# Batch 0 of a spectral mixer: transform products of two output thirds set around the token products, mirrored relus put off

## The chip, the cores and the metric

The kernel runs on one core of one Trainium2 chip. The metric is the device time of one execution in microseconds. The profile's span is about 2 us shorter than that time (592.4 against 594.3 for the kernel before, in the profiled execution); times of day within an execution ("at 32.17") count from the start of the span.

## The reference

For each of 8 batches of 3008 tokens by 256 channels: the real part of a 2-D Fourier transform, then a token-mixing and a channel-mixing perceptron, each with a residual.

```python
def _attn_ref(x):
    X = np.fft.fft(x, axis=1)
    X = np.fft.fft(X, axis=2)
    return X.real.astype(np.float32)

def _moe_ref(x, w_tok1, w_tok2, w_ch1, w_ch2):
    xt = x.transpose(0, 2, 1)
    h = np.maximum(xt @ w_tok1, 0.0) @ w_tok2      # 3008 -> 256 -> 3008
    u = x + h.transpose(0, 2, 1)
    h2 = np.maximum(u @ w_ch1, 0.0) @ w_ch2        # 256 -> 1536 -> 256
    return (u + h2).astype(np.float32)
```

## The kernel before

The instruction order of every engine is the order of the program text. A batch's columns are worked in six chunks of 512 (`NCH`). Three "thirds" of the transform `yt`, each good for one chunk and, mirrored, for another, are made by eight 128-column products each: four into `pq`, four into `py`. ScalarE copies `pq` to `qs`, and VectorE makes the two halves of `yt` from `py` and `qs` (I call this the join).

The program uses eight buffers of PSUM, where TensorE's products land, shared out as three rings: `f` (3), `mm` (3) and `o2` (2). A ring's buffer can be written again only when its last reader is done.

```python
    def ps_mm(name, dt=FP32, n=512):
        return psum.tile([P, n], dt, tag="mm", name=name, bufs=3)
    def ps_out(name, dt=FP32, n=512):
        return psum.tile([P, n], dt, tag="o2", name=name, bufs=2)
    def ps_f(name, dt=FP32, n=512):
        return psum.tile([P, n], dt, tag="f", name=name, bufs=3)
    # ... cut ...
        def relu(th, uv, which=(0, 1, 2)):
            for i in which:          # 1 and 2 are the mirrored ones, wanted from chunk 3 on
                o, x = ((uu[:, th, 0, :, :], uv[:]),
                        (uu[:, th, 1, :, 1:P], uv[:, :, 1:P]),
                        (uu[:, th, 1, :, 0], uv[:, ::-1, 0]))[i]
                nc.scalar.activation(out=o, in_=x, func=AFT.Relu)

        def third(c, then=None):
            py, pq = ps_f("py"), ps_f("pq")
            for o, f, tab in ((pq, 131, tq), (py, 1, tp)):
                for k in range(4):
                    g = 4 * c + k
                    nc.tensor.matmul(o[:, P * k:P * k + P], lhsT=w[:, g, f:f + P],
                                     rhs=tab[:, g, :], start=True, stop=True)
            qs = perb.tile([P, CW], FP32, tag="qs", name="qs", bufs=2)
            nc.scalar.activation(out=qs[:], in_=pq[:], func=AFT.Copy)
            # ... cut ...
            for h, op in ((0, AT.subtract), (1, AT.add)):
                nc.vector.tensor_tensor(out=yt[:, h, CW * c:CW * c + CW], in0=py[:],
                                        in1=qs[:], op=op)
        # ... cut: batch 0 makes third 0, tok1 and the first relus ...
        for c in range(NCH):
            if c in (1, 2):
                third(c)
                yield
            # ... cut ...
            if (b, c) == (0, 0):
                pus = [ps_f("pu") for _ in range(2)]
                # ... cut: identity products put yt into pus (start=True, stop=False) ...
                for th in range(2):
                    for h in range(2):
                        nc.tensor.matmul(pus[h][:], lhsT=uu[:, th, 0, h, :],
                                         rhs=w2_cols(b, c)[:, th],
                                         start=False, stop=(th == 1))
                for h in range(2):
                    copy(1 - h, ut[:, h, :]..., pus[h][:]...)   # h=0 VectorE, h=1 ScalarE
                for th in range(2):
                    relu(th, uvs[th], (1, 2))
                yield
                continue
            for h in range(2):       # every other chunk
                pu = ps_f("pu")
                # ... cut: two products (the token products) ...
                nc.vector.tensor_tensor(out=ut[:, h, 0:n]..., in0=pu[:, 0:n]..., in1=y..., op=AT.add)
                yield

    def mm1(b, c, c1, cts):          # a group of three channel tiles
        for i in cts:
            pc = ps_mm("pc")
            for h in range(2):
                nc.tensor.matmul(pc[:, 0:n], lhsT=wc[:, h, ct * P:(ct + 1) * P],
                                 rhs=ut[:, h, 0:n], start=(h == 0), stop=(h == 1))
            if i not in (2, 8) or (b, c) != (0, 0):
                nc.scalar.activation(out=c1[:, ct, 0:n], in_=pc[:, 0:n], func=AFT.Relu)
            else:                    # tiles 2 and 8 of chunk 0: VectorE
                ts(c1[:, ct, 0:n], pc[:, 0:n], 0.0, AT.max)
```

The main loop puts out a group `mm1` of three channel tiles, then a step (up to a `yield`) of the generator above, and so on. A step is, for instance, a third, or one token product pair `pu`.

## Time and profile before

| | kernel before |
|---|---|
| time, median of 3 runs | 594.20 us (594.19 to 594.73) |
| TensorE busy | 98% |
| VectorE, ScalarE, GpSimd busy | 77%, 74%, 26% |
| TensorE idle listed in the whole span | 8.1 us in six waits, 5.9 of it at the very start |
| of that on lines that the change touches | 0.52 us at 31.65 |

The lines that carry this are in the prediction. One more stretch of TensorE's timeline matters later: the fourth group of channel tiles, chunk 2's token products and the first group of chunk 1.

```profile
37.99 1.46 PE L773 MATMUL pc<-ut,wc1p 128*128 128x512 f16 x6
39.29 0.59 PE L730 MATMUL pu<-w2p,uu 128*128 128x512 f16 x2
39.72 1.46 PE L773 MATMUL pc<-ut,wc1p 128*128 128x512 f16 x6
...
41.44 1.47 PE L888 MATMUL po<-wc,c 128*128 128x256 f16 x12
```

Read such rows by their starts. The length of a row includes the modelled end of its last matmul and overlaps the next row by some 0.16 us. Six products cost 39.29 - 37.99 = 1.30 us, two with `w2p` 0.43 us.

### The profile page before, as it was taken

The numbers are of one execution on the slowest core, as the hardware profiler recorded it, in microseconds if no ns is written. First come the engines' busy times: TensorE is split into PE (matmuls) and PEld (weight loads), VectorE is DVE, ScalarE is ACT, GpSimd is POOL, SyncE is SP. The second block draws the span as 40 slices with busy tenths as digits, with TensorE's granted clock in tenths as the row PEclk, the third lists the DMA queues.
The fourth block names the chain that finished last, engine by engine and source line by source line (L and its number), as shares of the span: only waits on it lengthen the run. The fifth ranks groups of instructions, "written<-read, shape, count | busy, mean of one in ns | idle before, by whom it ended". The sixth has DMA issues, their size and how long they took to land.

```text
span 592.4 us, 15959 instructions
## 1 busy us (share of the span) xinstructions
PE 580.4 (98%) x6397; PEld 419.8 (71%) x6397; DVE 458.7 (77%) x1075; ACT 437.7 (74%) x994; POOL 152.7 (26%) x251
## 2 busy tenths in 40 slices
PE   5999999999999999999999999999999999999997
PEld 4846777767776777676777667767777777866676
DVE  8868689878896887769797787868888677676573
ACT  7775887887778777777767776777777867766772
POOL 7530421412151211421134111421211121112131
PEclk9999999999999999999999999999999999999999
DMA  9996851863367242844329432492233335333424
GB/s 151 211 187 126 139 101 46 150 122 54 66 122 139 55 88 56 157 71 98 64 49 170 98 65 55 90 172 54 56 76 63 78 55 97 48 72 72 82 58 105
DMA packets 86683, 56.55 MB, mean 95 GB/s; under 512 B 54945, under 2 KB 83553, under 8 KB 85857
## 3 DMA queue, kind: packets, MB, share of 16 engines
q1 hardware_dynamic: 77984, 37.77, 33.6%
q0 software_dynamic: 8320, 17.49, 17.2%
q8 instruction: 50, 0.82, 0.6%
q10 hardware_dynamic: 304, 0.26, 0.2%
q14 instruction: 25, 0.20, 0.1%
HBM read 34.98 MB, written 24.64 MB: 101 GB/s over the span
## 4 chain that ended last, share of the span: by engine, by line
PE 96%; DVE 2%; ACT 1%; issue 0%; POOL 0%; DVEq 0%; POOLq 0%
PE pc L773 41%; PE px L817 25%; PE py L817 10%; PE pu L730 7%; PE pt L613 4%; PE po L888 2%; PE pz L518 2%; PE pq L645 1%; PE py L645 1%; PE py L836 1%; PE pw L596 1%; PE pw L597 1%; PE pw L560 0%; ACT z L307 0%; PE ph L430 0%; PE ph L432 0%
## 5 line engine op out<-in xcount | busy, mean ns | idle before, releaser
L776 ACT ACTIVATE c<-pc 128x512 f16<-128x512 f32 (+1 forms) x574 | 297.9, 595 | 31.3 <-PE pc L773 16.3
L799 POOL TENSOR_TENSOR osb<-osb,rt 128x256 f32<-128x256 f32 (+1 forms) x92 | 84.5, 919 | 373.3 <-DVE osb L799 366.1
L817 PEld LDWEIGHTS <-c 128*128 128x128 f16 x2112 | 128.1, 98 | 24.9
L773 PE MATMUL pc<-ut,wc1p 128*128 128x512 f16 x576 | 140.0, 379 | 0.5 <-DVE ut L305 0.5
L773 PE MATMUL pc<-ut,wc1m 128*128 128x512 f16 (+1 forms) x576 | 134.9, 370 | 0.0
L822 ACT ACTIVATE m<-px 128x256 f32<-128x256 f32 (+1 forms) x138 | 51.8, 375 | 75.4 <-PE px L817 46.0
L817 PEld LDWEIGHTS <-sb 128*128 128x128 f16 x1584 | 94.6, 98 | 10.4
L738 DVE TENSOR_TENSOR ut<-pu,yt 128x512 f16<-128x512 f32 (+1 forms) x94 | 63.3, 674 | 40.6 <-PE pu L730 40.3
L773 PEld LDWEIGHTS <-wc1p 128*128 128x128 f16 x576 | 52.0, 97 | 49.2 <-DMA wc1p<-in_moe_w_ch_dram,ixc 0.8
L773 PEld LDWEIGHTS <-wc1m 128*128 128x128 f16 x576 | 52.9, 98 | 45.0
L817 PE MATMUL px<-wst,c 128*128 128x128 f16 x1056 | 74.0, 219 | 0.0
L817 PE MATMUL px<-wc,c 128*128 128x128 f16 x1056 | 66.5, 219 | 0.0
L799 DVE TENSOR_TENSOR osb<-py,m 128x256 f32<-128x256 f32 (+1 forms) x92 | 37.5, 407 | 26.5 <-ACT m L822 26.2
L790 DVE TENSOR_TENSOR sb<-sb,c 128x768 f16<-128x768 f16 (+1 forms) x92 | 54.2, 589 | 3.2
L730 PE MATMUL pu<-w2p,uu 128*128 128x512 f16 (+1 forms) x184 | 54.7, 379 | 0.0
L790 DVE TENSOR_TENSOR sb<-c 128x768 f16<-128x768 f16 (+1 forms) x92 | 50.6, 550 | 0.0
L790 DVE TENSOR_TENSOR c<-c 128x768 f16<-128x768 f16 (+1 forms) x92 | 50.5, 548 | 0.0
L790 DVE TENSOR_TENSOR sb<-c,sb 128x768 f16<-128x768 f16 (+1 forms) x92 | 50.4, 548 | 0.0
L307 ACT ACTIVATE z<-pz 128x480 f16<-128x480 f32 (+1 forms) x60 | 39.0, 666 | 5.4 <-PE pz L527 3.0
L599 DVE SCALAR_TENSOR_TENSOR w<-alt,pw 128x131 f16<-128x131 f16 x84 | 29.2, 351 | 16.5 <-ACT w L307 16.0
L652 DVE TENSOR_TENSOR yt<-py,qs 128x512 f16<-128x512 f32 x48 | 30.9, 685 | 10.5 <-ACT qs L648 10.2
L817 PE MATMUL py<-wst,sb 128*128 128x128 f16 x528 | 37.1, 219 | 0.0
(201 smaller groups left out, 648.1 us busy)
## 6 DMA issues: line engine op xcount, KB each, us to landing
out_dram<-osb SPq DMA_DIRECT2D x83, 256.0 KB, 3.8
xp<-in_x_dram POOLq DMA_DIRECT2D x16, 272.0 KB, 5.3
out_dram<-osb SPq DMA_DIRECT2D x11, 192.0 KB, 3.1
xp<-in_x_dram POOLq DMA_DIRECT2D x16, 127.5 KB, 5.8
rt<-ut SPq DMA_TRANSPOSE x96, 3.8
w2s<-in_moe_w_tok_dram POOLq DMA_DIRECT2D x1, 1504.0 KB, 14.8
w1p<-in_moe_w_tok_dram POOLq DMA_DIRECT2D x4, 192.0 KB, 7.9
wc<-in_moe_w_ch_dram POOLq DMA_DIRECT2D x1, 768.0 KB, 15.2
```

What stands on the lines that cost most here:

```text
L307: nc.scalar.activation(out=out_, in_=in_, func=AFT.Copy)
L599: nc.vector.scalar_tensor_tensor(out=w[:, g, 0:131], in0=alt[:], scalar=pw[:, 131:132], in1=pw[:, 0:131], op0=AT.mult, op1=AT.add)
L613: nc.tensor.matmul(pt[:, o:o + n], lhsT=hw[:, g, th * P:th * P + P], rhs=w[:, g, f:f + n], start=(g == 0), stop=(g == NG - 1))
L652: nc.vector.tensor_tensor(out=yt[:, h, CW * c:CW * c + CW], in0=py[:], in1=qs[:], op=op)
L730: nc.tensor.matmul(pu[:, 0:n], lhsT=uu[:, th, int(minus), h, :], rhs=w2_cols(b, c)[:, th], start=(th == 0), stop=(th == 1))
L738: nc.vector.tensor_tensor(out=ut[:, h, 0:n].rearrange("p (a b) -> p a b", b=64), in0=pu[:, 0:n].rearrange("p (b a) -> p a b", b=64), in1=y ...
L773: nc.tensor.matmul(pc[:, 0:n], lhsT=wc[:, h, ct * P:(ct + 1) * P], rhs=ut[:, h, 0:n], start=(h == 0), stop=(h == 1))
L776: nc.scalar.activation(out=c1[:, ct, 0:n], in_=pc[:, 0:n], func=AFT.Relu)
L790: nc.vector.tensor_tensor(out=o, in0=x, in1=y, op=op)
L799: eng.tensor_tensor(out=o, in0=x, in1=y, op=AT.add)
L817: nc.tensor.matmul(o[:, t], lhsT=a(k)[:, f:f + P], rhs=w(k), start=(first and t == 0 and k == 0), stop=(k == HC - 1), skip_group_check=True)
L822: nc.scalar.activation(out=m[:, i, t1], in_=pa[:, 0], func=AFT.Copy)
```

## The change

The intent: TensorE waits for the two copies of chunk 0's token products. Sixteen transform products of thirds 1 and 2 stand behind that wait and need nothing from it. So twelve go into it, and four ahead of the token products. Third 1 takes the two `o2` buffers, third 2 one `mm` and one `f` buffer. Third 2's join moves with its products, third 1's join stays. The mirrored relus, which stood on ScalarE where third 2's `qs` now stands, go to where third 2 was made.

```diff
--- before.py
+++ after.py
@@ -637,13 +637,21 @@
 
         yt = perb.tile([P, 2, HALF], FP16, tag="yt", name="yt")
 
+        def turn_part(c, o, part):
+            f, tab = ((131, tq), (1, tp))[part]
+            for k in range(4):
+                g = 4 * c + k
+                nc.tensor.matmul(o[:, P * k:P * k + P], lhsT=w[:, g, f:f + P],
+                                 rhs=tab[:, g, :], start=True, stop=True)
+            return o
+
         def third(c, then=None):
             py, pq = ps_f("py"), ps_f("pq")
-            for o, f, tab in ((pq, 131, tq), (py, 1, tp)):
-                for k in range(4):
-                    g = 4 * c + k
-                    nc.tensor.matmul(o[:, P * k:P * k + P], lhsT=w[:, g, f:f + P],
-                                     rhs=tab[:, g, :], start=True, stop=True)
+            turn_part(c, pq, 0)
+            turn_part(c, py, 1)
+            joined(c, py, pq, then)
+
+        def joined(c, py, pq, then=None):
             qs = perb.tile([P, CW], FP32, tag="qs", name="qs", bufs=2)
             nc.scalar.activation(out=qs[:], in_=pq[:], func=AFT.Copy)
             if then is not None:
@@ -694,7 +702,13 @@
         uts = st["ut"] = []
         for c in range(NCH):
             if c in (1, 2):
-                third(c)
+                if b:
+                    third(c)
+                elif c == 1:
+                    joined(1, *ahead[0])
+                else:
+                    for th in range(2):
+                        relu(th, uvs[th], (1, 2))
                 yield
             f0 = CW * c
             n = min(CW, S - f0)
@@ -711,6 +725,7 @@
                                      lhsT=ident[:],
                                      rhs=yt[:, h, 0:CW].rearrange("p (a b) -> p a b", b=64),
                                      start=True, stop=False)
+                pq = turn_part(1, ps_out("pq"), 0)
                 for th in range(2):
                     for h in range(2):
                         nc.tensor.matmul(pus[h][:], lhsT=uu[:, th, 0, h, :],
@@ -719,8 +734,9 @@
                 for h in range(2):
                     copy(1 - h, ut[:, h, :].rearrange("p (a b) -> p a b", b=64),
                          pus[h][:].rearrange("p (b a) -> p a b", b=64))
-                for th in range(2):
-                    relu(th, uvs[th], (1, 2))
+                ahead = [(turn_part(1, ps_out("py"), 1), pq)]
+                pq = turn_part(2, ps_mm("pq"), 0)
+                joined(2, turn_part(2, ps_f("py"), 1), pq)
                 yield
                 continue
             for h in range(2):
```

## The prediction

> **What bounds the kernel now.** I read the page's busy shares first, then what TensorE waited for over the whole run, then the timelines of TensorE, ScalarE and VectorE around the lines that the change touches. The page:
>
> ```profile
> PE 580.4 (98%) x6397; PEld 419.8 (71%) x6397; DVE 458.7 (77%) x1075; ACT 437.7 (74%) x994; POOL 152.7 (26%) x251
> ```
>
> TensorE is busy 98% of a 592.4 us span, so time can come only from fewer or cheaper matmuls, or from its holes. The change leaves the number of matmuls as it is: the order of the built instructions shows 12796 TensorE rows (loads and matmuls) in both kernels, 1006 VectorE rows, 642 ScalarE rows. So only holes are left. This is the complete answer to what TensorE waited for:
>
> ```profile
> PE filler L294 <- DVE altu L325: 5.9, 1, 5.9
> PE pz L518 <- ACT tt L287: 0.6, 1, 0.6
> PE pc L773 <- DVE ut L305: 0.5, 1, 0.5
> PE pw L560 <- ACT tt L307: 0.4, 1, 0.4
> PE pz L518 <- DVE xp L488: 0.4, 1, 0.4
> PE pt L265 <- ACT tq L252: 0.3, 1, 0.3
> ```
>
> The columns are total us, times and the longest. Only the third row is on lines that the change touches; the others lie before 19 us. After about 32.2 us no hole is listed at all. TensorE's timeline at that hole (start, length, and in brackets the idle time before and its releaser):
>
> ```profile
> 29.58 1.02 PE L710 MATMUL pu<-yt,ident 128*128 128x512 f16 x2
> 30.40 1.25 PE L716 MATMUL pu<-w2s,uu 128*128 128x512 f16 x4
> 32.17 1.46 PE L773 MATMUL pc<-ut,wc1p 128*128 128x512 f16 x6 [0.52 <-DVE ut L305]
> 33.46 0.39 PE L645 MATMUL pq<-tq,w 128*128 128x128 f16 x4
> 33.68 0.39 PE L645 MATMUL py<-tp,w 128*128 128x128 f16 x4
> ...
> 37.54 0.39 PE L645 MATMUL pq<-tq,w 128*128 128x128 f16 x4
> 37.77 0.39 PE L645 MATMUL py<-tp,w 128*128 128x128 f16 x4
> ```
>
> The token products of chunk 0 (four at L716) must be copied out of PSUM before the first channel product (L773) can read `ut`. TensorE has nothing to do meanwhile. The 16 small transform products of thirds 1 and 2 stand behind that hole, four by four. The two copies, the relus and the later joins:
>
> ```profile
> 31.68 0.60 ACT L307 ACTIVATE ut<-pu 128x512 f16<-128x512 f32 x1 [1.07 <-PE pu L716]
> 32.18 0.90 ACT L636 ACTIVATE uu<-uv 128x254 f16<-128x254 f32 x4
> 32.98 1.07 ACT L776 ACTIVATE c<-pc 128x512 f16<-128x512 f32 x2
> 33.93 0.60 ACT L648 ACTIVATE qs<-pq 128x512 f32<-128x512 f32 x1
> ```
>
> ```profile
> 31.42 0.69 DVE L305 CAST ut<-pu 128x512 f16<-128x512 f32 x1 [1.16 <-PE pu L716]
> 33.72 0.69 DVE L97 TENSOR_SCALAR c<-pc 128x512 f16<-128x512 f32 x1 [1.60 <-PE pc L773]
> 34.57 1.29 DVE L652 TENSOR_TENSOR yt<-py,qs 128x512 f16<-128x512 f32 x2 [0.16 <-ACT qs L648]
> ```
>
> VectorE's copy ends at 32.11 and the first channel product starts 0.06 us later, at 32.17. That is the release.
>
> **What the Trainium skill says.** "TensorE: Matmul & The Clock Gate", section "Back-to-back issue gap", gives for a warm stream a gap of N/2.4 + 2.5 ns: 56 ns for 128 columns and 216 ns for 512. The trace agrees: the four at L645 take 0.22 us to the next group (33.46 to 33.68, so 55 ns each), and six at L773 take 33.46 - 32.17 = 1.29 us (215 ns each). The page's sustained 81 and 131 ns do not fit these rows. "Perfetto Trace Analysis", section "Tensor Engine Instruction (MATMUL, LD_WEIGHTS)", says that the end of a matmul is computed from its size, not seen. So the 0.52 us counts from a modelled end, 31.65. Counted by issue, the last of the four L716 products starts at about 31.22 and costs 0.265 us (two of them at L730 with the same operand take 34.43 - 33.91 = 0.52 us), so TensorE could have issued again at 31.49: the usable hole is 32.17 - 31.49 = 0.68 us. "ScalarE: Activation LUTs", section "What ACT_TABLE_LOAD costs", gives 186 ns + 0.833 ns an element for an activation with immediates, with 93 ns of overlap back to back: 612 ns for 512 columns, one every 520. The trace has 0.60 us, one every 0.50 (31.68 to 32.18). I use the trace's.
>
> **The change, part by part.**
>
> 1. Four products of third 1 (the `pq` half) go between the identity products and the token products. The identity products are issued out by about 30.36, and their successor starts at 30.40; `uu` of the first half was ready at 29.94. There is no hole to fill there. So these four delay the token products, both copies and the first channel product by 4 x 55 = 0.22 us: 32.17 becomes 32.39.
> 2. The other twelve (third 1 `py`, third 2 `pq` and `py`) go behind the token products: 12 x 55 = 0.66 us, from 31.49 + 0.22 = 31.71 to 32.37. They fit into the hole, which now ends at 32.39, and leave 0.02 us.
> 3. All 16 leave their old places at 33.46 and 37.54: 16 x 55 = 0.88 us less there.
>
> Sum on TensorE: 0.88 - 0.22 = 0.66 us off the path, if nothing new makes it wait. It is the same 0.66 as the twelve that fall into the hole.
>
> 4. New waits. The third channel product's buffer is the one of third 2's `pq`, so it waits for the ScalarE copy `qs`. That starts when the `ut` copy lets go, 32.18 + 0.22 = 32.40, and ends at 33.00. The product is due at 32.39 + 4 x 0.215 = 33.25. It fits by 0.2 us.
> 5. VectorE now makes third 2's `yt` (1.29 us) before its relu of the third channel tile. It begins at about 33.06 and passes on at 34.27; the relu ends at 34.96. The sixth channel product needs that buffer at 32.39 + 1.30 + 0.53 + 0.86 = 35.08. It fits by about 0.1 us.
> 6. The mirrored relus (0.90 us, one after the other 0.80) move from 32.18 to behind the eighth channel tile, where the 0.50 us of `qs` stood. There ScalarE is at work without a hole. I put the relus at 37.61 to 38.41, then three channel relus, one every 0.50, ending at about 39.00, 39.50 and 40.00. The first products of chunk 1 want these three buffers at about 39.08, 39.52 and 39.97 on the earlier clock. That is a shortfall of some 0.05 us on the last two. I take 0.06 us for it, and up to 0.04 for point 5.
>
> Net: 0.66 - 0.06 to 0.10 = about 0.6 us, that is 0.1% of 594.2. Behind it TensorE has no hole up to its end, so the gain should travel to the end undiminished: 594.2 - 0.6 = 593.6 us.
>
> **The rivals.**
>
> A: the hole is held by something else as well, a transfer. The weight loader's row names the arrival of the channel weights' second half for 0.8 us before L773, and its transfer took 16.2 us from an issue at 15.8, so it lands near 32.0. If landing, and not the copy, held the product, the fill would still remove products from later, and the start could not move earlier. The change does not need it to: it starts later, at 32.39, so this rival costs nothing. Against it being the cause: the product follows the copy by 0.06 us.
>
> B: the moved work makes ScalarE or VectorE the bound for some us (points 4 to 6 each have a margin of 0.2 us or less). If all three were 0.2 us worse than I put them, about 0.3 us of the gain would be left: 593.9. For it speaks the thin margin; against it, that the token products of chunks 1 and 2 sit between the channel tiles and give both engines time.
>
> C: the gain is made and then given back, because something with its own clock meets TensorE later. The gather for batch 1 lands near 44.7 and VectorE waits 1.35 us for it there; the transposed `rt` also lands at 45.7. Neither becomes earlier, so VectorE keeps its old time for the next few us while TensorE is 0.6 ahead. But TensorE needs VectorE's results of that stretch only later: the block sums end at about 55.1 and their product starts at 56.4, a margin of 1.3 us before and 0.7 after. I give this 15%, and it would leave 594.0 to 594.2.
>
> D: the inserted four hide in a hole that I do not see. Then the gain would be up to 0.88: 593.3.
>
> **Range and chances.** The effects span 593.3 (D) to 594.2 (C). The three times of the kernel before lie from 594.19 to 594.73, so noise of a tenth of a per cent is as large as the effect. I say 593.6, with 593.1 to 594.3 for 8 in 10. To be faster by over 2% it would have to save 12 us, more than all holes after the start together; to be slower by as much, it would have to open holes of 12 us. Neither has a path.
>
> **What the profile of the changed kernel would show.** Step 1: first channel product at about 32.4, not 32.2. Step 2: the wait of the channel product on the `ut` copy gone or below 0.1 us, with the twelve products between. Step 3: chunk 1's first channel products (39.72 before) at 39.1 to 39.2. Steps 4 to 6: no row of TensorE waiting for `qs`, for the VectorE relu or for ScalarE's relus above 0.1 us. Last: the final output products, at 583.09 before, at about 582.5. The prediction is wrong if a new TensorE wait of 0.3 us or more shows between 32 and 60 us, if the first channel product is still 0.5 us from the product before it, or if the 0.6 us is there at 39 us and gone at 583.

## The result

| | before | changed |
|---|---|---|
| median of 6 runs | 594.28 us (594.19 to 595.54) | 593.60 us (593.57 to 593.71) |
| span of the profiled run | 592.4 us | 591.9 us |

The ratio is 0.9984 (95% interval 0.9972 to 0.9997). It is the mean time of one kernel's fast runs over that of the other's in the same rounds, so not quite the ratio of the medians (0.9989): one run of the kernel before at 595.54 is in the mean. By the medians the change saves 0.68 us.

This is the complete answer to what TensorE waited for in the changed kernel:

```profile
PE filler L294 <- DVE altu L325: 5.9, 1, 5.9
PE pz L518 <- ACT tt L287: 0.6, 1, 0.6
PE pw L560 <- ACT tt L307: 0.4, 1, 0.4
PE pz L518 <- DVE xp L488: 0.4, 1, 0.4
PE pt L265 <- ACT tq L252: 0.3, 1, 0.3
```

The row of the channel product is gone; the other five are as before. TensorE's timeline from the identity products to the first output products (L644 is now the line of the transform products, L731 and L746 of the token products, L789 of the channel products, L904 of the output products):

```profile
29.60 1.02 PE L724 MATMUL pu<-yt,ident 128*128 128x512 f16 x2
30.42 0.43 PE L644 MATMUL pq<-tq,w 128*128 128x128 f16 x4
...
31.73 0.38 PE L644 MATMUL py<-tp,w 128*128 128x128 f16 x4
...
32.41 1.46 PE L789 MATMUL pc<-ut,wc1p 128*128 128x512 f16 x6
...
36.05 2.83 PE L789 MATMUL pc<-ut,wc1p 128*128 128x512 f16 x12
38.72 0.59 PE L746 MATMUL pu<-w2p,uu 128*128 128x512 f16 x2
39.15 1.51 PE L789 MATMUL pc<-ut,wc1p 128*128 128x512 f16 x6
40.50 0.59 PE L746 MATMUL pu<-w2p,uu 128*128 128x512 f16 x2
40.93 1.47 PE L904 MATMUL po<-wc,c 128*128 128x256 f16 x12
```

The twelve products fill 31.73 to 32.41 without a gap. The first channel product starts at 32.41, against 32.17 before. Then the sixteen are missing further on, and the first output products start at 40.93, against 41.44.

I use one measure for every kernel here: **the path**, from the first identity product to the first output product. The same products lie in it in every kernel, whatever their order. Before, it is 41.44 - 29.58 = 11.86 us; changed, 40.93 - 29.60 = 11.33 us. So 0.53 us were saved there, not the 0.66 that went into the hole. Two small waits took the rest, and neither is in the list of waits:

- The twelve channel products from 36.05 should cost 12 x 0.2155 = 2.59 us and end at 38.64; the next row starts at 38.72. Narrow windows of the timeline show two delays. The ninth product starts at 37.81 and was due at 37.77; its buffer is the one that ScalarE's relu of tile 7 reads. The eleventh starts at 38.29 and was due, behind the ninth, at 38.25; its buffer is the one that VectorE's relu of tile 8 reads:

```profile
37.17 0.59 ACT L792 ACTIVATE c<-pc 128x512 f16<-128x512 f32 x1
```

```profile
37.54 0.69 DVE L97 TENSOR_SCALAR c<-pc 128x512 f16<-128x512 f32 x1 [0.22 <-PE pc L789]
```

The relus end at 37.76 and 38.23, and each time the product starts 0.05 us later: 0.04 us lost twice, 0.08 in all. Nothing stands between the third and the fourth group any more, because the step between them now holds only relus.

- The six products from 39.15 take 40.50 - 39.15 = 1.35 us in place of 1.29: 0.06 us lost behind the put-off relus, which ScalarE did from 37.65, ahead of the three channel relus that these products' buffers wait for:

```profile
37.65 0.91 ACT L636 ACTIVATE uu<-uv 128x254 f16<-128x254 f32 x4
```

0.66 - 0.08 - 0.06 = 0.52 us, and 0.53 is measured.

At the end of the run the final output products start at 582.51, against 583.09: 0.58 us earlier, 0.60 by the clock of the first identity product. The missing 0.07 came back near 110 us. There, in the kernel before, TensorE's timeline:

```profile
110.21 0.50 PE L817 MATMUL px<-wst,c 128*128 128x128 f16 x6
110.62 0.49 PE L817 MATMUL py<-wc,sb 128*128 128x128 f16 x6
```

The six products at `px` take 0.41 us to the next row; in the changed kernel the same two rows start at 109.70 and 110.04, 0.34 apart. VectorE's read of `py` runs from 110.30 to 110.58 before, and `py` is written again from 110.62. In the changed kernel VectorE does that read from 109.56 to 109.84, early enough. It got ahead because its join of batch 1's third starts at 104.99 there and at 105.71 before; why by more than TensorE's half microsecond I did not follow further.

### The profile page after: what moved, and what is told of

Read it like the earlier page. It is cut to its first block, busy times and chain, and to the rows that moved or that the text cites. A ratio compares the mean times of both kernels' runs of the same rounds, so it can differ in the third digit from the quotient of the medians.

```text
span 591.9 us, 15955 instructions
## 1 busy us (share of the span) xinstructions
PE 580.3 (98%) x6397; PEld 419.9 (71%) x6397; DVE 458.8 (78%) x1075; ACT 437.8 (74%) x994; POOL 152.8 (26%) x251
## 3 DMA queue, kind: packets, MB, share of 16 engines
q1 hardware_dynamic: 77984, 37.77, 34.7%
## 4 chain that ended last, share of the span: by engine, by line
PE 96%; DVE 2%; ACT 1%; issue 0%; POOL 0%; DVEq 0%; POOLq 0%
PE pc L789 41%; PE px L833 25%; PE py L833 10%; PE pu L746 7%; PE pt L613 4%; PE po L904 2%; PE pz L518 2%; PE py L644 1%; PE pq L644 1%; PE py L852 1%; PE pw L596 1%; PE pw L597 1%; PE pw L560 0%; ACT z L307 0%; PE ph L432 0%; PE ph L430 0%
## 5 line engine op out<-in xcount | busy, mean ns | idle before, releaser
L789 PE MATMUL pc<-ut,wc1p 128*128 128x512 f16 x576 | 140.0, 379 | 0.0
L789 PE MATMUL pc<-ut,wc1m 128*128 128x512 f16 (+1 forms) x576 | 134.9, 370 | 0.0
L789 PEld LDWEIGHTS <-wc1p 128*128 128x128 f16 x576 | 52.0, 97 | 48.6 <-issue 1.2
L789 PEld LDWEIGHTS <-wc1m 128*128 128x128 f16 x576 | 52.9, 98 | 45.0
L746 PE MATMUL pu<-w2p,uu 128*128 128x512 f16 (+1 forms) x184 | 54.7, 379 | 0.0
```

The lines of the kernel that those rows point to most:

```text
L746: nc.tensor.matmul(pu[:, 0:n], lhsT=uu[:, th, int(minus), h, :], rhs=w2_cols(b, c)[:, th], start=(th == 0), stop=(th == 1))
```

## The experiments

Seven kernels, all with correct results, each timed in 5 rounds. Every edit is against the changed kernel unless it says otherwise. "Path" is the measure above, less that of the kernel before. "Time" is the difference of the medians in the same rounds.

| kernel | path, us | time, us | median, us |
|---|---|---|---|
| changed | -0.53 | -0.68 | 593.60 |
| relus back | +0.40 | +0.33 | 594.55 |
| relus put off only | +0.35 | +0.35 | 594.57 |
| all 16 behind the token products | -0.55 | -0.63 | 593.59 |
| relus at chunk 3 | -0.67 | -0.75 | 593.47 |
| relus later on ScalarE only | -0.60 | -0.66 | 593.54 |
| third 2 only in the hole | -0.07 | -0.05 | 594.15 |
| third 1 only in the hole | -0.44 | -0.46 | 593.74 |

The path and the medians give the same order, but for the two slowest, which lie within 0.05 us of each other. The intervals of the ratios, some 0.0027 wide (1.6 us), are wider than any of these differences, because single runs of several kernels lie 1.1 to 1.5 us high (see the last section). So the reading rests on the medians and, above all, on the traces.

### Relus back at their old place (e1_relus_back)

```diff
-                else:
-                    for th in range(2):
-                        relu(th, uvs[th], (1, 2))
                 yield
 # ... behind the two copies of chunk 0:
+                for th in range(2):
+                    relu(th, uvs[th], (1, 2))
                 ahead = [(turn_part(1, ps_out("py"), 1), pq)]
```

> The changed kernel with the mirrored relus back at once behind the chunk 0 copy. My theory (the putting off is needed, because the copy qs of third 2 now stands in that place of ScalarE's queue and frees the third channel product's buffer): qs starts 0.80 us later, at about 33.2; the third channel product, due at 33.27, waits to about 33.9 (0.6 us), and the sixth waits about 0.15 us for VectorE; the start of chunk 2's first token product lies 0 to 0.2 us after the kernel before (39.29), and the time is 594.2 to 594.5. Rival (only the filling of the hole counts, the relus' place does not): no wait, 38.6 to 38.7, and 593.6.

Measured: 594.55 us, 0.33 slower than before. In its list of TensorE's waits two rows are new against the changed kernel on lines of the change:

```profile
PE pc L788 <- ACT qs L656: 0.4, 1, 0.4
PE pc L788 <- ACT c L791: 0.3, 1, 0.3
```

By starts the first is 0.58 us: four products from 33.91 are through at 34.77, and the fifth starts at 35.35. That is the expected wait for `qs`. The second is 0.42 us (due 37.17, started 37.59), where I had expected 0.15 us for VectorE. The built order tells why: in this kernel the pool (the part of the program that hands out the PSUM buffers when it is built) gave the sixth channel tile the buffer of the fourth tile, not of the third, so it waits for ScalarE's relu of the fourth, as the second row says. With the 0.07 us at the adjacent groups: 0.66 - 0.58 - 0.42 - 0.07 = -0.41 us, and the path is 0.40 us longer. So the putting off of the relus is needed once third 2's products stand in the hole: without it the whole gain is lost. Of the loss, 0.58 us is the relus' own; 0.42 is the pool's other choice of buffer, which came with them.

### Relus put off, nothing else (e2_relus_only)

The edit is against the kernel before:

```diff
                 third(c)
+                if b == 0 and c == 2:
+                    for th in range(2):
+                        relu(th, uvs[th], (1, 2))
                 yield
 # ... behind the two copies of chunk 0:
-                for th in range(2):
-                    relu(th, uvs[th], (1, 2))
                 yield
```

> The kernel before with nothing but the mirrored relus put off, behind third 2's qs. My theory (the relus did not hold TensorE where they stood): the 0.52 us wait of the first channel product stays, no gain; at their new place they push three channel relus back by 0.8 us and open TensorE waits of 0.3 to 0.4 us at 39.7 to 41; time 594.5 to 594.7. Rival (the relus early on ScalarE were what cost time): 0.3 us or more faster than before, 594.0 or less.

Measured: 594.57 us, 0.35 slower. TensorE, at the hole and at the new place of the relus:

```profile
32.15 1.46 PE L774 MATMUL pc<-ut,wc1p 128*128 128x512 f16 x6 [0.52 <-DVE ut L305]
...
39.26 0.59 PE L731 MATMUL pu<-w2p,uu 128*128 128x512 f16 x2
39.93 1.56 PE L774 MATMUL pc<-ut,wc1p 128*128 128x512 f16 x6
```

The hole is untouched. At the new place 39.93 - 39.26 - 0.43 = 0.24 us are lost, and, as the next row starts at 41.33, another 41.33 - 39.93 - 1.29 = 0.11 us, 0.35 in all. Putting the relus off gains nothing by itself and costs at its new place.

### All sixteen behind the token products (e3_all_behind)

```diff
-                pq = turn_part(1, ps_out("pq"), 0)     # ahead of the token products
 # ... behind the two copies of chunk 0:
+                pq = turn_part(1, ps_out("pq"), 0)
                 ahead = [(turn_part(1, ps_out("py"), 1), pq)]
```

> The changed kernel with the four third 1 products that stand ahead of the token products put behind them too, so that all 16 fall between the token products and the first channel product. My theory (those four gain nothing ahead: they push the token products by the 0.22 us that they save later): the token products end 0.22 us earlier, 16 products need 0.88 us in a hole of 0.68, the first channel product starts at 32.4 all the same, and the time is that of the changed kernel, 593.6, within 0.05. Rival (the four ahead cover a wait of the token products on their relu, as the placing suggests): 0.1 to 0.22 us slower, 593.7 to 593.8.

Measured: 593.59 us, as the changed kernel.

```profile
31.49 0.39 PE L644 MATMUL pq<-tq,w 128*128 128x128 f16 x4
...
32.39 1.46 PE L789 MATMUL pc<-ut,wc1p 128*128 128x512 f16 x6
```

The first four follow the token products at 31.49, 0.24 us earlier than `py` did, and the channel product starts at 32.39 all the same: now the sixteen hold it up, not the copies. What does not fit into the hole moves the start by as much as it saves later. The four ahead are neutral.

### Relus at the head of chunk 3 (e4_relus_chunk3)

```diff
-            if c in (1, 2):
+            if c in (1, 2) and b or c in (1, 3) and not b:
```

The step with the relus alone now comes two steps later, and chunk 2's first token products stand between the third and the fourth group.

> The changed kernel with the mirrored relus put off further, to the head of chunk 3, without the empty step that they held, so that chunk 2's first token products come between the third and the fourth group of channel products again. My theory (the trace of the changed kernel shows the sixth product of that stretch 0.08 us late, held by VectorE's relu, because nothing stands between the two groups, and another 0.06 us late behind the put-off relus): both go; third chunk's products lie 0.12 us earlier than in the changed kernel, the time is about 593.5. Rival (these small waits are swallowed later, as 0.07 us came back near 110 us): 593.6.

Measured: 593.47 us, the fastest kernel here.

```profile
36.03 1.46 PE L789 MATMUL pc<-ut,wc1p 128*128 128x512 f16 x6
37.33 0.59 PE L746 MATMUL pu<-w2p,uu 128*128 128x512 f16 x2
37.76 1.46 PE L789 MATMUL pc<-ut,wc1p 128*128 128x512 f16 x6
```

The groups take 1.29 or 1.30 us again (the next rows start at 39.05, 39.48 and 40.78, the last with the output products). The path is 0.67 us shorter than before, all of what goes into the hole, and the final output products start at 582.37, 0.14 before the changed kernel's. So the small waits were real time and were not swallowed later. (The text on record puts the 0.08 us down to VectorE's relu alone; half of it was ScalarE's, as shown under the result.)

### Relus later on ScalarE only (e5_relus_later)

```diff
-                else:
-                    for th in range(2):
-                        relu(th, uvs[th], (1, 2))
                 yield                                  # an empty step stays
 # ... behind the token products of chunk 2, second half:
+                if (b, c, h) == (0, 2, 1):
+                    for th in range(2):
+                        relu(th, uvs[th], (1, 2))
```

> The changed kernel with only the mirrored relus' place on ScalarE moved, behind chunk 2's second token products, where ScalarE has over 1 us idle; the empty step between the third and fourth group of channel products stays, so TensorE's order is that of the changed kernel. My theory (two separate small waits: 0.08 us because nothing stands between those two groups and VectorE's relu frees the buffer too late, and 0.05 to 0.06 us from the relus on ScalarE): the first stays, chunk 2's first token product at 38.7 as in the changed kernel; the second goes, the second one at 40.45 in place of 40.50; time 593.5 to 593.6. Rival (both waits come from the put-off relus): both go, 38.65 and 40.38, and 593.47 as with the relus at chunk 3.

Measured: 593.54 us.

```profile
36.10 2.83 PE L789 MATMUL pc<-ut,wc1p 128*128 128x512 f16 x12
38.77 0.59 PE L743 MATMUL pu<-w2p,uu 128*128 128x512 f16 x2
...
40.49 0.59 PE L743 MATMUL pu<-w2p,uu 128*128 128x512 f16 x2
```

(This run's identity products start at 29.66, 0.06 late.) The twelve products still take 38.77 - 36.10 = 2.67 us, 0.08 too many; the six after them, from 39.20 to 40.49, take 1.29 again. So the two waits are separate: the adjacent groups make the first, the relus' place on ScalarE the second.

### Third 2 only in the hole (e6_third2_only)

```diff
-                pq = turn_part(1, ps_out("pq"), 0)
-                ahead = [(turn_part(1, ps_out("py"), 1), pq)]
 # ... at chunk 1:
-                    joined(1, *ahead[0])
+                    third(1)
```

> The changed kernel with only third 2's eight products set into the hole; third 1's eight stay behind the first three channel tiles, as in the kernel before. My theory (the gain is the products that fall into the hole, 55 ns each): the first channel product starts at 32.17 with about 0.1 us or less of listed wait (8 x 0.055 = 0.44 of 0.68 us filled), 0.44 less the same two small waits of 0.13 us is 0.3 us at the second token product of chunk 2; time about 593.9. Rival (the gain comes from taking the joins out of ScalarE's and VectorE's way, of which third 2's is the one that matters): the full gain, 593.6.

Measured: 594.15 us. The expected 0.3 us was not there: the path is 0.07 us shorter.

```profile
33.67 0.39 PE L644 MATMUL py<-tp,w 128*128 128x128 f16 x4
34.13 0.69 PE L744 MATMUL pu<-w2s,uu 128*128 128x512 f16 x2
```

The channel product starts at 32.15, and the hole keeps 0.24 us, as expected. But the token product due at 33.89 starts at 34.13. Third 1 takes two `f` buffers here, so the token product gets the third one, which holds third 2's `py`. VectorE's join read it from 32.79 for 1.29 us, to 34.08. So 0.44 - 0.24 (this wait) - 0.08 - 0.06 = 0.06 us. My theory's term for the products held; I had overlooked the buffer. The rival, that third 2's join is what matters, falls: its join is early here, and the gain is a tenth of a microsecond.

### Third 1 only in the hole (e7_third1_only)

```diff
-                pq = turn_part(1, ps_out("pq"), 0)     # ahead of the token products
 # ... behind the two copies of chunk 0:
+                pq = turn_part(1, ps_out("pq"), 0)
                 ahead = [(turn_part(1, ps_out("py"), 1), pq)]
-                pq = turn_part(2, ps_mm("pq"), 0)
-                joined(2, turn_part(2, ps_f("py"), 1), pq)
+                for th in range(2):
+                    relu(th, uvs[th], (1, 2))
 # ... at chunk 2, in place of the put-off relus:
+                    third(2)
```

> A cleaner half dose than with third 2, whose eight products gained only 0.05 us because their buffer was wanted again by chunk 1's first token product: now third 1's eight products alone go into the hole, in the two output buffers that the change gives them; third 2 stays where the kernel before has it, and the mirrored relus too. My theory (the gain is 55 ns for each product in the hole, and no buffer is wanted early here): first channel product at 32.17 with some 0.24 us of hole left, then 8 x 0.055 = 0.44 us earlier than the kernel before at chunk 2's first token product (38.85), and 593.8. Rival (a half-filled hole gains next to nothing, as the third 2 run showed, because the pipe needs all of the change): 594.1 to 594.2.

Measured: 593.74 us, 0.46 us faster than before; the path is 0.44 us shorter, which is 8 x 55 ns. Half the fill without a new wait gives its full worth, so the gain does not need the whole change. It needs products in the hole and a free buffer for what follows. This run differs from the one before in more than the buffer: the groups of channel tiles stay apart and the relus stay at their old place. Of the 0.37 us between the two paths 0.24 is the wait for the buffer, the rest are the two small waits.

## Why the prediction was right

593.6 was said, 593.60 measured; the range held it. The mechanism was as said, the last digit is luck: the gain is 0.68 us by the medians, because the kernel before stood at 594.28 and not at 594.20 in these rounds, and 0.60 us by the traces. Point by point:

- **Only holes can be gained.** Right: TensorE's busy time is 580.3 us against 580.4, and the one row that left the list of waits is that of the channel product. (The prediction's counts of built rows, 12796, 1006 and 642, stand in no view kept here. The pages count 6397 matmuls and 6397 weight loads, 1075 instructions on VectorE and 994 on ScalarE, in both kernels alike, and that is what the step needs.)
- **The size of the hole by issue, 0.68 us, not the listed 0.52.** Right. The relus at chunk 3, with no other wait, save 0.67 us of path: more than the listed idle time.
- **Steps 1 to 3: four ahead are neutral, twelve fill, 0.66 us.** Right. The channel product starts at 32.41 (32.39 said), and with all sixteen behind the result is the same.
- **Steps 4 and 5, `qs` and the join by VectorE fit by 0.2 and 0.1 us.** Right: `qs` ends at 33.01, and the second group keeps its 1.29 us (34.23 to 35.52). That the fit is what counts was shown by putting the relus back.
- **Step 6, up to 0.06 us behind the put-off relus.** Right, 0.06 us.
- **What it missed.** One term was absent: the third and the fourth group of channel tiles become neighbours, and ScalarE's relu of tile 7 and VectorE's of tile 8 then free their buffers too late, for 0.08 us in all. The 0.04 us that I held ready for step 5 did not occur. So the predicted net of 0.56 to 0.60 us would have been 0.52 on the path, as measured, and the 0.60 us at the end of the run rest on the 0.07 us that came back near 110 us, which nobody foresaw.
- **The rivals.** A (the transfer of the channel weights) cost nothing: that row's landing could not hold a product that starts at 32.41. B (ScalarE or VectorE as the bound) happened at 0.14 us, less than its 0.3. C (given back later) did not happen; the opposite did, by 0.07. D (a hole ahead of the token products) fell with all sixteen behind.

## What to carry to other kernels

Size a hole by when TensorE could have issued again, and move into it no more than fits: the surplus only changes places. For every product moved, ask which buffer it now holds and who wants that buffer next; half of this change gained 0.05 us where a buffer was wanted early (a wait of 0.24 us) and two small waits stayed, and 0.46 us where neither was so. And look at what the moved work used to separate: two groups that become neighbours can outrun a ring of three buffers.

## What the Trainium skill lacked or had wrong

- "TensorE: Matmul & The Clock Gate", "Back-to-back issue gap": its isolated formula (the page's word; the prediction says "for a warm stream") holds in this real kernel (55 ns measured against 56 for 128 columns, 215 against 216 for 512); its sustained 81 and 131 ns do not.
- The same section has one cost for each width and none for how the moving operand lies in SBUF. Here 512 columns are read as 64 runs of eight: from `w2s`, where the runs lie 47 columns apart, a product costs some 263 ns (33.91 to 34.43 and 35.72 to 36.25 for two each, kernel before), and from the copy `w2p`, where they lie 48 apart, 215 ns. That the alignment of the runs is the cause was not tested.
- "Perfetto Trace Analysis", "Tensor Engine Instruction (MATMUL, LD_WEIGHTS)", says that the end of a matmul is computed, but not what follows for reading waits: the hole of 0.68 us is listed as 0.52, and waits of 0.04, 0.06 and 0.24 us are not listed at all. Row starts against the count of products show them.
- No page that I looked up gives the time in which a PSUM buffer comes round. Here, for a 512-column tile: two products issued at 36.91, VectorE's relu 37.54 to 38.23, next product at 38.29, so 1.38 us. Three buffers of two products each cover 3 x 0.43 = 1.29 us.
- No page that I looked up says that a pool may hand out its buffers in another order when an instruction elsewhere moves: the relus put back changed the buffer of the sixth channel tile and cost 0.42 us.
- No page that I looked up is concerned with the single high runs: the kernel before had 595.54, 595.36 and 595.63 in two of four sets of rounds, other kernels 595.32 and 596.07. The last one was a profiled run, and there alone TensorE waited for the first token weights, in this row:

```profile
PE ph L432 <- DMA w1m<-in_moe_w_tok_dram: 1.2, 1, 1.2
```

  The identity products start at 31.11 there, 1.5 us late, before anything that the change touches. That the other high runs have the same cause is not shown.
